# The lo parts of tiles 4 to 7 of the second norm made by GpSimd, with a search of 63 rounds for the order

## The chip, the cores and the metric

The kernel runs on one core of a Trainium2 chip. The metric is the device time of one execution in microseconds (us). The kernel before takes 686.99 us, the median of three runs (686.92 to 687.37). One execution was recorded by the hardware profiler; it took 687.41 us, of which the recorded span is 685.7.

## The reference

One transformer layer on 2048 tokens of width 448: attention over a sliding window of 256 tokens with 16 heads of 28, behind a layer norm, and a gated feed-forward part of inner width 1792, behind a second layer norm. Both are added to what came in.

```
q, k, v = split(layernorm(x) @ wqkv)            # 16 heads of 28
s = q @ k.T * 28**-0.5                          # kept where 0 <= i - j < 256
h = x + concat(softmax(s) @ v) @ wo             # first residual
n = layernorm(h)                                # the second norm
out = h + (gelu(n @ w_gate) * (n @ w_up)) @ w_down
```

All of it is float32.

## The kernel before

**Products.** TensorE multiplies numbers in a rounded float32 form. Each operand is therefore split into a hi part, the value rounded to that form, and a lo part, the rest; a product is the sum of hi by hi, hi by lo and lo by hi. ScalarE makes a hi part by a copy (`to_hi`, L498). VectorE or GpSimd makes the lo part by a subtraction (`to_lo`, L501). All split products are recorded at one line, L495.

**Stages.** The tokens lie in 16 tiles of 128, and `hres` holds the residual stream, which becomes h and then the output. After the first norm and the projections comes attention, in two passes over the heads and 16 blocks of 128 tokens in each: products of scores (L495), maxima on VectorE (`scores`, L924), exponentials on ScalarE (`probs`, L996), the mask on GpSimd (`select`, L1007), products with the values (`attend`, L1026), the division by the sums (`drain`, L1049, on GpSimd in some blocks), the split of a block's output into hi and lo (into `ohl`), its product with `wo`, and the residual add into `hres` (L1073). Blocks end one after the other, and while the later ones are still at work, the second norm of the earlier tiles and the first products of the feed-forward part begin.

**The second norm** (`layer_norms` L515, `normalise` L542, `turn` L583). For each tile VectorE takes the statistics (L530, L532), ScalarE normalises (L548), VectorE transposes in 32 by 32 blocks (L587), and four DMAs on SyncE's queue write the tile to DRAM so that it comes out transposed (L591; the buffers are called xn_122 for tile 0, xn_123 for tile 1, and so on, xn_126 for tile 4 and xn_127 for tile 5). For tiles 0 to 7 two more DMAs bring it back into `xT` (L595, L597), ScalarE makes its hi part (L601 to L603) and an engine its lo part, in two subtractions: 128 by 3 by 128, and 64 by 128 for the last 64 rows of the width, whose hi part is kept in a piece of `ring`. That engine is GpSimd for the tiles listed in `TURNED`, VectorE otherwise (L599). Tiles 8 to 15 are not split there.

**The first products.** `conv` (L1305) makes one inner tile of 128 features for 512 tokens: products of `xT` with weights in `proj`, a gelu (L1339) on ScalarE and a product with the up part (L1341) on VectorE, which goes into `v` and `mt` and is split in turn. `FIRST` lists the eight of these that come first. The pairs in it are (c, k), c the group of 512 tokens: c = 0 needs tiles 0 to 3, c = 1 needs tiles 4 to 7. `down` (L1278) multiplies the results with the down weights and adds them to `hres` (L1296), four tiles a step.

**The units.** The other products go by a scheme with fewer multiplications: `unit` (L1222) uses sums and differences of tiles and of weights. `combine` (L648) makes the combined inputs: it loads transposed tiles from DRAM into `v` (L674), adds or subtracts two of them (L693), and splits the result into hi (ScalarE) and lo (VectorE, X at L501). Its weights come from DRAM, already or not yet combined, and `record` (L1147) handles them, with DMAs at L1157 and L1158 and sums on GpSimd (L1164).

**What sets the order.** No engine's row is written by hand. Each operation is given to a planner (class `Lists`) with its engine, an estimated cost, what it reads and writes, and a key. `run` simulates six queues (TensorE, VectorE, ScalarE, GpSimd, SyncE and a bookkeeping one) and picks on each the operation that can go next by its key. `refine` (L337) repeats this `ROUNDS` times from a fixed random seed: it changes the keys at random, or by how late each operation may start, plans again, and keeps the best by its own estimate. The order kept is then issued. The cost of a lo part in that estimate depends on its engine (L611): 1.6 on GpSimd, 0.75 on VectorE. Another cost or engine for one operation, or another number of rounds, gives another order nearly everywhere. PSUM has eight banks, which the planner hands out as well; in the rows below they are bank_138 to bank_145.

Of the kernel before, what the change touches and what calls it, by code (L numbers as in the profile page):

```python
# [51 lines left out]
POOLED = (3,)  # L52
PKX = (2, 3)
MOVED = 0
TURNED = (0, 1, 2, 3)
LN2 = (120, 10)
XK = ((0, 10), (240, 10))
ADDS = ("dve", "dve")
# [14 lines left out]
    return max(n / 2400 + 0.004, 0.112)  # L73


ROUNDS = 110
SEED = 3
HEAT = 0.3
MIX = 0.8
# [17 lines left out]
class Lists:  # L97
# [6 lines left out]
    def op(self, eng, cost, lat, key, fn, r=(), w=(), bank=None, port=False, size=0, tag=None, after=()):  # L104
        o = Op()
        o.eng, o.cost, o.lat, o.key, o.fn, o.port, o.size, o.tag = eng, cost, lat, key, fn, port, size, tag
        o.deps, o.users, o.ready, o.start = set(after), [], 0.0, None
        o.banks = () if bank is None else tuple(bank) if type(bank) is list else (bank,)
        for b in o.banks:
            b.left += 1  # L110
        if eng == "pe":
            w = (*w, *o.banks)
        else:
            r = (*r, *o.banks)
        for toks, wr in ((r, False), (w, True)):
            for tok in toks:
                name, lo, hi = tok if type(tok) is tuple and tok[0] in SPANS else (tok, 0, 1)
                old = self.seen.setdefault(name, [])
                keep = []
                for a in old:  # L120
                    if a[0] < hi and lo < a[1] and a[2] is not o:
                        if wr or a[3]:
                            o.deps.add(a[2])
                        if wr and lo <= a[0] and a[1] <= hi:
                            continue
                    keep.append(a)
                keep.append((lo, hi, o, wr))
                self.seen[name] = keep
        for d in o.deps:
            d.users.append(o)  # L130
        self.ops.append(o)
        if tag is not None:
            self.open[tag] = self.open.get(tag, 0) + 1
            self.all.setdefault(tag, []).append(o)
        return o
# [201 lines left out]
    def refine(self, allowed, idle):  # L337
# [8 lines left out]
        kept = keys = [o.key for o in self.ops]  # L346
        for r in range(ROUNDS):
            kind = rnd.random()
# [28 lines left out]
def block_kernel(ctx: ExitStack, tc, x, wqk_in, wv_in, wo_in, ffn_in, halves_in, out):  # L377
# [77 lines left out]
    def span(name, lo, n):  # L455
        return (name, lo, lo + n)
# [18 lines left out]
    def XT(t):  # L475
        return span("xT", t, 1)
# [106 lines left out]
    def turn(t, key):  # L583
# [14 lines left out]

        eng = nc.gpsimd if t in TURNED else nc.vector  # L599

# [5 lines left out]
        def lo():  # L606
# [3 lines left out]
        op("act", 0.7, 0.82, key + 0.2, hi, [("xt3", t)], [XT(t), span("ring", 10240, 128)])  # L610
        op("pool" if t in TURNED else "dve", 1.6 if t in TURNED else 0.75, 1.7 if t in TURNED else 0.82, key + 0.2, lo,  # L611
           [XT(t), span("ring", 10240, 128)], [XT(t)], port=True)
# [1021 lines left out]
```

## Time and profile before

| what | us |
|---|---|
| median of three runs | 686.99 (686.92 to 687.37) |
| the profiled execution | 687.41 |
| its span | 685.7 |
| TensorE busy | 673.9 (98%), 4079 products |
| VectorE busy | 502.4 (73%) |
| ScalarE busy | 419.6 (61%) |
| GpSimd busy | 296.8 (43%) |

Attention ends some 280 us into the span; the first early product of the feed-forward part starts shortly before, the units run from about 400 us to the end. In the rows, L and a number is a line of the kernel, x and a number a count of instructions, PE is TensorE, DVE is VectorE, ACT is ScalarE, POOL is GpSimd, and SPq is the time in which SyncE's queue held a transfer back. In a row of a timeline the first number is the start in us and the second the busy time of the whole row; what stands in brackets is a wait ahead of it and what ended it. In a row of groups of instructions the three numbers after the count are the shortest, middle and longest in ns, and then the time from the first to the last in us. A list of waits gives the total in us, the count and the longest.

### The profile page before, as it was taken

Reading aid. Unit: us, or ns where it says so; the run is one execution under the profiler, and the core shown is the slowest. Engines: PE = TensorE matmul, PEld = TensorE weight load, DVE = VectorE, ACT = ScalarE, POOL = GpSimd, SP = SyncE. Lnnn points to the kernel's source line nnn. Section 1 sums busy time; section 2 is a strip of 40 time slices with the busy share of each in tenths; the row PEclk is TensorE's granted clock in tenths of the full one; section 3 lists DMA queues with packets and bytes.
Section 4 is the critical chain, followed back from the end, with each engine's and each line's share of the span. In section 5 each row is a group of like instructions: output and inputs, shape, how many; then the busy total and the mean of one; then the engine's idle time right before and its main releaser. Section 6 shows DMA issues by size and latency. Waiting matters only on the chain.

```text
span 685.7 us, 12258 instructions
## 1 busy us (share of the span) xinstructions
PE 673.9 (98%) x4079; PEld 593.4 (87%) x4079; DVE 502.4 (73%) x1274; ACT 419.6 (61%) x908; POOL 296.8 (43%) x462
## 2 busy tenths in 40 slices
PE   8999999999999999999999999999999999999997
PEld 8898888888888877677898899899999999999997
DVE  7968978866587867784899998877667745645544
ACT  7758767777766789696655665644554543533331
POOL 5702544344445668546524465254664631501100
PEclk9999999999999999999999999999999999999999
DMA  8798765566547687633533432212212210111102
GB/s 290 229 307 264 225 186 177 165 191 197 174 149 221 171 245 195 168 74 85 148 91 101 116 110 75 86 53 76 66 53 90 67 53 14 39 53 67 54 1 107
DMA packets 92951, 89.67 MB, mean 131 GB/s; under 512 B 35224, under 2 KB 82008, under 8 KB 92888
## 3 DMA queue, kind: packets, MB, share of 16 engines
q1 hardware_dynamic: 92888, 88.89, 43.4%
q8 instruction: 32, 0.52, 0.3%
q14 instruction: 31, 0.25, 0.1%
HBM read 59.51 MB, written 29.36 MB: 130 GB/s over the span
## 4 chain that ended last, share of the span: by engine, by line
PE 86%; DVE 7%; ACT 3%; DMA 3%; issue 1%; POOL 0%; SPq 0%; DVEq 0%; ACTq 0%
PE bank L495 79%; PE bank L1026 6%; DMA v<-xn 1%; ACT ring L498 1%; PE bank L553 1%; DVE proj L501 1%; DVE v L693 1%; DVE X L501 1%; DVE mt L924 1%; DVE hres L1296 1%; DMA q<-proj 1%; ACT proj L498 1%; ACT xT L498 1%; ACT pp L996 1%; DVE bnst L530 0%
## 5 line engine op out<-in xcount | busy, mean ns | idle before, releaser
L495 PE MATMUL bank<-xT,proj 128*128 128x512 f32 x620 | 178.9, 387 | 0.0
L495 PE MATMUL bank<-ring 84*128 84x384 f32 (+5 forms) x618 | 155.4, 314 | 2.6 <-ACT pp L996 1.5
L924 DVE CUSTOM_DVE_ANT_0 mt<-bank,mt 128x384 bf16<-128x384 f32 (+2 forms) x256 | 129.0, 526 | 36.9 <-PE bank L495 31.9
L996 ACT ACTIVATE pp<-bank 128x384 f32<-128x384 f32 (+2 forms) x352 | 123.6, 390 | 45.1 <-PE bank L495 41.7
L495 PE MATMUL bank<-xT,ring 128*128 128x512 f32 x536 | 134.9, 380 | 0.1
L495 PEld LDWEIGHTS bank<-ring 104*128 104x128 f32 (+2 forms) x618 | 109.8, 191 | 25.6 <-issue 5.6
L495 PE MATMUL bank<-ring,proj 128*128 128x448 f32 x628 | 127.5, 353 | 1.6 <-DVE hres L1296 1.6
L1007 POOL TENSOR_SCALAR_AFFINE_SELECT pp<-pp 128x512 f32<-128x512 f32 x120 | 74.9, 638 | 117.2 <-ACT pp L996 106.1
L495 PEld LDWEIGHTS bank<-xT,proj 128*128 128x128 f32 x620 | 114.4, 191 | 10.8 <-issue 0.6
L495 PEld LDWEIGHTS bank<-ring,proj 128*128 128x128 f32 x628 | 118.6, 189 | 4.6 <-ACT xT L498 1.9
L495 PEld LDWEIGHTS bank<-xT,ring 128*128 128x128 f32 x536 | 100.9, 189 | 13.5 <-DVE v L1240 0.5
L1296 DVE TENSOR_TENSOR hres<-bank,hres 128x448 f32<-128x448 f32 x72 | 41.3, 622 | 26.8 <-PE bank L495 26.7
L495 PE MATMUL bank<-proj,xT 128*128 128x224 f32 x352 | 59.9, 275 | 0.2 <-ACT proj L498 0.2
L1258 ACT ACTIVATE v<-v 128x512 f32<-128x512 f32 x24 | 15.2, 632 | 69.5 <-DVE v L1240 69.5
L501 POOL TENSOR_TENSOR ring<-raw,ring 128x256 fp32r<-128x256 f32 (+2 forms) x42 | 38.3, 921 | 42.1 <-ACT ring L498 34.3
L495 PEld LDWEIGHTS bank<-proj,xT 128*128 128x128 f32 x352 | 53.2, 191 | 1.5 <-ACT proj L498 0.4
L1164 POOL TENSOR_TENSOR v<-raw 128x256 f32<-128x256 f32 x18 | 15.4, 856 | 89.8 <-DMA raw<-in_halves_dram 54.9
L495 PE MATMUL bank<-wos,ohl 128*128 128x448 f32 x192 | 50.2, 363 | 0.0
L501 DVE TENSOR_TENSOR proj<-v,proj 128x512 fp32r<-128x512 f32 (+1 forms) x56 | 43.0, 773 | 8.6 <-ACT proj L498 7.4
L498 ACT ACTIVATE proj<-v 128x512 fp32r<-128x512 f32 (+1 forms) x56 | 33.6, 603 | 24.3 <-DVE v L1266 13.4
L495 PE MATMUL bank<-X,ring 128*128 128x512 f32 x146 | 48.2, 379 | 0.0
L1164 POOL TENSOR_TENSOR raw<-raw 64x128 f32<-64x128 f32 (+1 forms) x90 | 46.1, 525 | 2.2
(116 smaller groups left out, 987.5 us busy)
## 6 DMA issues: line engine op xcount, KB each, us to landing
ring<-k SPq DMA_DIRECT2D x44, 336.0 KB
raw<-in_halves_dram SPq DMA_DIRECT2D x18, 640.0 KB
ring<-q SPq DMA_DIRECT2D x32, 336.0 KB
q<-proj SPq DMA_DIRECT2D x15, 448.0 KB
k<-proj SPq DMA_DIRECT2D x11, 448.0 KB
hres<-in_x_dram SPq DMA_DIRECT2D x16, 224.0 KB
xn<-xn SPq DMA_DIRECT2D x64, 56.0 KB
mt<-in_halves_dram SPq DMA_DIRECT2D x16, 224.0 KB
```

The source lines that it names most:

```text
L495: nc.tensor.matmul(o.rearrange("p (t h) -> p t h", h=2), w, mixed(m), **how)
L498: nc.scalar.activation(dst, src, AF.Copy)
L501: (eng or nc.vector).tensor_sub(dst, src, f(hi))
L553: nc.tensor.transpose(bank[b.k][:, n * 128:(n + 1) * 128], xn[i2][:, o:o + 128], ident)
L693: op("dve", 0.07 + n * 0.00104, 0.17 + n * 0.00104, key, lambda: nc.vector.tensor_tensor(out, a, b, op=op_), [*ar, *br, "mtfree"], w, port ...
L924: nc.vector.tensor_tensor_reduce(plain(junk[s % 2][:, o:384]), unmixed(bank[b.k][:, o:384]), plain(mask[:, o:384]), 1.0, -BIG, OP.add, OP. ...
L996: nc.scalar.activation(plain(pp[:, j, o * 128:o * 128 + n]), unmixed(bank[b.k][:, 0:n]), AF.Exp, scale=SCALE)
L1007: nc.gpsimd.affine_select(a, a, pattern=[[0, 4], [-cm, 128]], compare_op=op_, fill=0.0, base=0, channel_multiplier=cm)
L1026: nc.tensor.matmul(bank[b.k][32 * j:32 * j + DH + 1, lo * 128:(hi + 1) * 128], v[:, 4 * c - 2 + m, g % 2, j, :], pp[:, j, at[m] * 128:(at[ ...
L1164: op("pool", 0.14 + n * 0.00215, 0.18 + n * 0.00215, key, lambda: nc.gpsimd.tensor_tensor(out, a, b, op=OP.subtract), [*ar, *br], w, port= ...
L1258: op("act", 0.485, 0.608, key + 11, lambda: nc.scalar.activation(A, A, AF.Gelu_apprx_tanh), ta, ta)
L1296: op("dve", 0.533, 0.626, key + 3 * q + 3, lambda t=t, b=banks[q]: nc.vector.tensor_tensor(plain(hres[:, t, :]), unmixed(bank[b.k][:, 0:D] ...
```

## The change

The list of tiles whose lo part GpSimd makes grows from tiles 0 to 3 to tiles 0 to 7, and the search for the order has 63 rounds and not 110.

```diff
@@ -52,7 +52,7 @@
 POOLED = (3,)
 PKX = (2, 3)
 MOVED = 0
-TURNED = (0, 1, 2, 3)
+TURNED = (0, 1, 2, 3, 4, 5, 6, 7)
 LN2 = (120, 10)
@@ -73,7 +73,7 @@
-ROUNDS = 110
+ROUNDS = 63
 SEED = 3
```

Eight instructions change their engine: the two subtractions of tiles 4, 5, 6 and 7. None is added or taken away. The order changes on every engine; the three places on which the prediction rests follow.

GpSimd at the end of attention, before. `pp` are the exponentials, `oblk` a block's output, `ohl` its split:

```order
L1007 AFFINE_SELECT pp<-pp 128x4x128 x3
L1049 TENSOR_TENSOR oblk<-oblk,rcp_87 128x512
L1007 AFFINE_SELECT pp<-pp 128x4x128 x2
L501 TENSOR_TENSOR ohl<-oT,ohl 128x512
L1007 AFFINE_SELECT pp<-pp 128x4x128 x5
```

And the same place of the changed kernel:

```order
L1007 AFFINE_SELECT pp<-pp 128x4x128 x4
L1049 TENSOR_TENSOR oblk<-oblk,rcp_87 128x512
L1007 AFFINE_SELECT pp<-pp 128x4x128 x2
L501 TENSOR_TENSOR xT<-xT 128x3x128
L501 TENSOR_TENSOR xT<-xT,ring 64x128
L501 TENSOR_TENSOR ohl<-oT,ohl 128x512
L1007 AFFINE_SELECT pp<-pp 128x4x128 x2
L501 TENSOR_TENSOR xT<-xT 128x3x128
L501 TENSOR_TENSOR xT<-xT,ring 64x128
```

The lo parts of tiles 4 and 5 now stand between the selections. Those of tiles 6 and 7 follow further down in the same manner, tile 7's between two selections of the last block; VectorE's row has none of the four pairs left.

VectorE at the first step of `down`, before. The adds at L1073 are the last residual adds of attention, `v` and `mt` at L1341 the products with the up part, and `proj<-v,proj` the lo part of the first such product:

```order
L1073 TENSOR_TENSOR hres<-bank_144,hres 128x448
L1341 TENSOR_TENSOR v<-v 128x512 x2
L1073 TENSOR_TENSOR hres<-bank_142,hres 128x448
L1073 TENSOR_TENSOR hres<-bank_145,hres 128x448
L1341 TENSOR_TENSOR mt<-bank_139,mt 128x512
L1073 TENSOR_TENSOR hres<-bank_144,hres 128x448
L530 BN_STATS bnst_80<-hres 128x6
L501 TENSOR_TENSOR proj<-v,proj 128x512
```

And in the changed kernel:

```order
L1073 TENSOR_TENSOR hres<-bank_144,hres 128x448
L1341 TENSOR_TENSOR v<-v 128x512 x2
L1073 TENSOR_TENSOR hres<-bank_145,hres 128x448
L501 TENSOR_TENSOR proj<-v,proj 128x512
L1073 TENSOR_TENSOR hres<-bank_142,hres 128x448
L1073 TENSOR_TENSOR hres<-bank_144,hres 128x448
L1341 TENSOR_TENSOR mt<-bank_139,mt 128x512
L530 BN_STATS bnst_80<-hres 128x6
L532 BN_AGGR bnmv<-bnst_80 128x2
L501 TENSOR_TENSOR proj<-v,proj 128x512
```

The first lo split stands behind one residual add there and not behind three adds, a product and a statistics step; the second split stands where the first one stood.

SyncE, on which all DMAs are issued, at the loads for the first combined inputs, before:

```order
L674 DMA v<-xn_126 64x128
L674 DMA v<-xn_126 128x2x128
L1158 DMA v<-in_halves_dram 128x448
L674 DMA v<-xn_126 64x2x128
L674 DMA v<-xn_127 64x128
L674 DMA v<-xn_122 64x2x128
L674 DMA v<-xn_122 128x2x128
L674 DMA v<-xn_127 128x2x128
L1157 DMA raw<-in_halves_dram 128x1280
L674 DMA v<-xn_126 64x2x128
L674 DMA v<-xn_127 64x2x128
L674 DMA v<-xn_122 64x2x128
```

And in the changed kernel:

```order
L674 DMA v<-xn_126 64x128
L674 DMA v<-xn_126 128x2x128
L1158 DMA v<-in_halves_dram 128x448
L674 DMA v<-xn_122 64x2x128
L674 DMA v<-xn_122 128x2x128
L674 DMA v<-xn_126 64x2x128
L674 DMA v<-xn_127 64x128
L674 DMA v<-xn_127 128x2x128
L674 DMA v<-xn_122 64x2x128
```

The third load of tile 0 (the last row of both) stands ahead of the weight record (L1157), which comes five rows further down in the changed kernel.

## The prediction

> **What bounds the kernel now.** I read the page first: the engines' totals, and the chain that ended last.
>
> ```profile
> span 685.7 us, 12258 instructions
> PE 673.9 (98%) x4079; PEld 593.4 (87%) x4079; DVE 502.4 (73%) x1274; ACT 419.6 (61%) x908; POOL 296.8 (43%) x462
> PE 86%; DVE 7%; ACT 3%; DMA 3%; issue 1%; POOL 0%; SPq 0%; DVEq 0%; ACTq 0%
> ```
>
> TensorE is the bound: 98% busy and 86% of the chain. The change takes no product away, so it can gain only where TensorE stands still or runs slowly. Where that is, TensorE's own waits and a table by stage tell.
>
> ```profile
> PE bank L495 <- DVE proj L501: 1.7, 1, 1.7
> PE bank L495 <- DVE hres L1296: 1.6, 1, 1.6
> PE bank L495 <- ACT pp L996: 1.5, 4, 0.8
> 275.00:280.00 5.00, 3.95 (x21) 2.65 (x18) 4.86 (x20) 3.37 (x11) 4.32 (x7) 1.00 0.98 285
> 280.00:284.00 4.00, 4.00 (x15) 3.29 (x14) 1.76 (x9) 1.38 (x4) 1.84 (x5) 0.57 1.00 234
> 284.00:300.00 16.00, 16.00 (x118) 12.29 (x118) 13.52 (x46) 14.13 (x38) 6.62 (x9) 1.00 0.34 74
> 300.00:320.00 20.00, 19.71 (x140) 15.48 (x143) 11.26 (x26) 17.18 (x44) 13.20 (x21) 1.00 0.33 63
> 320.00:340.00 20.00, 18.34 (x106) 16.59 (x99) 15.87 (x31) 10.30 (x17) 7.91 (x11) 1.00 0.56 158
> 340.00:360.00 20.00, 20.00 (x99) 18.36 (x98) 18.75 (x52) 12.24 (x24) 7.64 (x14) 1.00 0.32 85
> 360.00:380.00 20.00, 18.42 (x91) 16.68 (x90) 18.91 (x43) 10.43 (x18) 7.71 (x11) 1.00 0.40 107
> 400.00:560.00 160.00, 160.00 (x780) 146.79 (x778) 121.00 (x209) 85.50 (x156) 82.26 (x128) 1.00 0.23 72
> ```
>
> After each stage and its length stand the busy times of TensorE, its weight loads, VectorE, ScalarE and GpSimd, and then the granted clock. Four things are to be seen. The second half runs without a gap (160.00 of 160). Two single waits of 1.7 and 1.6, both for VectorE, lie in 320 to 340 and 360 to 380. At the end of attention TensorE misses 1.05 in 275 to 280, with VectorE busy 4.86 of 5 and GpSimd 4.32, and right behind it the clock is 0.57 over 4 us: (1 - 0.57) x 4 = 1.7 us lost. And in 284 to 320, where VectorE still makes the lo parts of tiles 4 to 7, TensorE misses 0.29.
>
> **The change part by part.** *The moved lo parts.* Each is two subtractions; their prices on both engines:
>
> ```profile
> L501 POOL TENSOR_TENSOR xT<-xT x4: 1002/1004/1009, 241.4 to 277.1; 128x384 fp32r<-128x384 f32 x4
> L501 POOL TENSOR_TENSOR xT<-xT,ring x4: 454/456/462, 242.5 to 278.2; 64x128 fp32r<-64x128 f32 x4
> L501 DVE TENSOR_TENSOR xT<-xT x4: 547/552/559, 294.7 to 310.9; 128x384 fp32r<-128x384 f32 x4
> L501 DVE TENSOR_TENSOR xT<-xT,ring x4: 290/290/318, 295.3 to 311.5; 64x128 fp32r<-64x128 f32 x4
> ```
>
> VectorE loses 4 x (0.55 + 0.29) = 3.4 us and GpSimd gains 4 x (1.00 + 0.46) = 5.8. Both fall in 290 to 312. VectorE is busy there 13.52 of 16 and 11.26 of 20, so its release is worth at most the 0.29 that TensorE misses. GpSimd goes from 6.62 + 13.20 = 19.8 busy of 36 to 25.6: room on the average. In the new order ScalarE's hi part of tile 4 comes ahead of the last hi split of block 13's output, and the lo part stands behind two selections, so GpSimd need not idle for it. Only at the end is it tight, with tile 7:
>
> ```profile
> 311.51 0.29 DVE L501 TENSOR_TENSOR xT<-xT,ring 64x128 fp32r<-64x128 f32 x1
> ...
> 312.76 1.56 PE L495 MATMUL bank<-xT,proj 128*128 128x512 f32 x6
> ```
>
> The lo part ends at 311.80 and its first product starts at 312.76: 0.96 of cover, of which the slower engine takes (1.00 + 0.46) - (0.55 + 0.29) = 0.6. I cost this at nothing; if GpSimd's queue is late by more than 0.36, the products of tiles 4 to 7 are the next thing late. Ends: -0.3 (VectorE's release counts) and +5.8 (all four lo parts on the path).
>
> *The stretch before the first early product.* The new search moves nearly every row. Ahead of the lo part of tile 3, which that product waits for, stand the same GpSimd instructions in both orders, only in another sequence; TensorE has two score products more ahead of the early product. So I take 0. Its ends: -1.05 - 1.7 = -2.7, if wait and slow clock both go, and as much to the other side.
>
> *The start.* There the trace shows VectorE's steps up to the lo part of tile 3:
>
> ```profile
> 9.12 0.69 DVE L501 TENSOR_TENSOR proj<-raw,proj 128x512 fp32r<-128x512 f32 x1
> ...
> 10.74 0.63 DVE L530 BATCH_NORM_STATS2 bnst<-hres 128x6 f32<-128x448 f32 x1
> ```
>
> The new order has a second such weight split ahead of it and not this statistics step: +0.06, taken as 0. Ends: one such step either way, 0.7.
>
> *The first wait of the feed-forward part.* Here the order bears more than the moved work does.
>
> ```profile
> 329.10 0.35 PE L495 MATMUL bank<-proj 128*128 128x448 f32 x1
> 331.11 2.73 PE L495 MATMUL bank<-proj 128*128 128x448 f32 x13 [1.66 <-DVE proj L501]
> 326.44 1.28 DVE L1341 TENSOR_TENSOR v<-v 128x512 f32<-128x512 f32 x2
> 327.64 1.15 DVE L1073 TENSOR_TENSOR hres<-bank,hres 128x448 f32<-128x448 f32 x2
> ...
> 329.30 0.62 DVE L1073 TENSOR_TENSOR hres<-bank,hres 128x448 f32<-128x448 f32 x1
> ...
> 330.37 0.68 DVE L501 TENSOR_TENSOR proj<-v,proj 128x512 fp32r<-128x512 f32 x1
> 327.50 1.14 ACT L498 ACTIVATE proj<-v 128x512 fp32r<-128x512 f32 x2
> ```
>
> The second product of the first down step waits for a lo split that VectorE starts at 330.37, behind three residual adds, a product and a statistics step. Its hi part on ScalarE is done about 328.1. In the new order the split stands right behind the first add: that add ends near 328.2, the split takes 0.68 and is done at 328.9, ahead of the product at 329.1. What is late next is that step's first bank: it now belongs to the add behind the split, which ends at 328.9 + 0.6 = 329.5. So 0.4 of the wait stays, and 0.1 comes at the second step, whose split now has a product and a statistics step less of a head start: -1.66 + 0.5 = -1.2. Ends: -1.66, and -0.6 if ScalarE's part is late by one of its steps of 0.6.
>
> *The second wait.* VectorE is behind here (18.75 and 18.91 of 20):
>
> ```profile
> 361.37 2.43 PE L495 MATMUL bank<-ring,proj 128*128 128x448 f32 x12
> 365.38 2.51 PE L495 MATMUL bank<-ring,proj 128*128 128x448 f32 x12 [1.58 <-DVE hres L1296]
> 363.29 0.42 DVE L501 TENSOR_TENSOR X<-v,xT 128x256 fp32r<-128x256 f32 x1
> 363.62 0.48 DVE L693 TENSOR_TENSOR v<-v 64x128 f32<-64x128 f32 x2
> ...
> 364.63 2.20 DVE L1296 TENSOR_TENSOR hres<-bank,hres 128x448 f32<-128x448 f32 x4
> 334.14 0.60 SPq L674
> ...
> 334.80 4.82 DMA v<-xn
> ...
> 339.63 0.64 ACT xT L498
> 340.36 0.63 DVE L501 TENSOR_TENSOR X<-v,xT 128x128 fp32r<-128x128 f32 x2 [2.11 <-ACT xT L498]
> ```
>
> The four residual adds of a down step start at 364.63, some 2.4 after the first three of the twelve products (361.37 + 0.6 + drain). Three changes meet. Five VectorE steps stand behind these adds now and not ahead (the three shown, 0.9 together, and two more of that size: 1.5). The wait of 2.11 at 340.36 is for the combined input of tile 0, whose last transfer SyncE issued at 334.14. Its buffer is free when the lo split above is done, now 328.9 and not 331.05; and the new order issues this transfer ahead of the 640 KB weight record, not behind it. I take 1.7 of the 2.11 as saved (ends 0 and 2.11). Against these, TensorE comes 1.2 earlier. VectorE is then 2.4 - 1.5 - 1.7 + 1.2 = 0.4 late, which the other nine products cover. But the five steps are still owed before the first unit's products, and VectorE has no other slack: together the two waits can give little more than the 1.7 it saves and 0.2 of play. So the second gives 1.9 - 1.2 = 0.7 of its 1.58. Ends: 0, -1.58.
>
> *Behind.* 0: the next 160 us hide everything.
>
> **Sum**: 0 + 0 + 0 - 1.2 - 0.7 = -1.9. The profiled execution took 687.41 (685.7 and 1.7 around it): 685.5. It lies 0.4 above the median of the runs, 686.99, which gives **685.1**.
>
> **The rivals.** *Slower: GpSimd's queue.* The lo parts stand ahead of selections, and every attend product waits for selections. For it: GpSimd takes 1.46 for each, in order. Against it: GpSimd now mostly waits for the exponentials. If two of the four come onto the path, 2 x 1.46 = 2.9; TensorE then waits longer than the 1.05 after which the clock fell, and I add another 1.7 for that: 687.0 - 1.9 + 2.9 + 1.7 = 689.7. It decides from 1.9 us of added wait.
>
> *No change.* The transfer of 4.82 takes as long in its new place, and VectorE's wait stays. What is gained at 329 is then waited for at 365: 687.0.
>
> *More gain: the clock.* TensorE fell to 0.57 after missing 1.05 of 5 us in several pieces, and did not after the single waits of 1.66 and 1.58. If the new order fills 275 to 280 better, 1.7 goes too: 687.0 - 1.9 - 1.7 = 683.4. [...]
>
> **How the numbers follow.** Forecast 0.45 (with its ends 683.6 to 686.6), slower 0.23, no change 0.17, clock 0.15. The range 682.6 to 689.4 takes in the clock case and most of the slow one, and leaves out the sums of all ends. A change below 0.2% (1.4 us) is about what a measurement of this kernel cannot tell. Faster by more: three quarters of the forecast and the clock case, 0.34 + 0.15 = 0.49. Within: 0.11 of the forecast and 0.15 of no change, 0.26. Slower: the rest, 0.25.
>
> **What would show it.** In the changed profile: TensorE's wait for the split of the first down step at most 0.5; VectorE's wait before the first combined input below 1; no wait of more than 0.9 for the residual adds; TensorE's miss in the 36 us of tiles 4 to 7 still below 0.5; one slow stretch of the clock. I am wrong if attend products wait for GpSimd, if the products of tiles 4 to 7 start late, or if the slow stretch comes twice or not at all.

## The result: slower, by the order and not by the engine

The changed kernel takes 690.19 us (689.82 to 691.26), the kernel before 686.99 (686.02 to 687.37) beside it: 3.2 us more by the medians. The ratio is 1.0055, with a 95% interval of 1.0040 to 1.0071, or 3.8 us (2.7 to 4.9). The forecast was 685.1, the range 682.6 to 689.4.

The head of the page of the changed kernel's profiled execution (690.96 us, span 689.2):

```profile
span 689.2 us, 12270 instructions
PE 677.1 (98%) x4077; PEld 592.6 (86%) x4077; DVE 497.9 (72%) x1266; ACT 420.5 (61%) x908; POOL 307.0 (45%) x470
PE 84%; DVE 7%; ACT 3%; DMA 2%; issue 2%; SPq 1%; DVEq 0%; ACTq 0%
```

VectorE lost 4.5 us of work and GpSimd gained 10.2 (its count grew by 8), where 3.4 and 5.8 were forecast. In the two experiments below that take the change apart, the moved work alone gives GpSimd 5.4 more (302.2 us), and the new order alone 5.0 more with the same instructions (301.8 us). TensorE is the bound as before. Its waits, as total, count and longest:

```profile
PE bank L495 <- DVE mx L924: 1.6, 6, 0.4
PE bank L951 <- DVE mhl L944: 1.3, 2, 0.7
PE bank L495 <- DVE xT L501: 0.9, 1, 0.9
PE bank L495 <- DVE hres L1296: 0.8, 1, 0.8
PE bank L495 <- DVE hres L1073: 0.3, 1, 0.3
```

The wait of 1.7 for the split of the first down step is gone and the one of 1.6 for the residual adds is halved, as forecast. The waits for maxima (mx) grew from 0.6 in two pieces to 1.6 in six. New are those for VectorE's small step behind the maxima (mhl) and one for a lo part of the first norm (xT at the top of the kernel). The table by stage, with the columns of the prediction (length; busy time of TensorE, weight loads, VectorE, ScalarE, GpSimd; granted clock; DMA share and rate):

```profile
275.00:280.00 5.00, 4.72 (x42) 3.39 (x41) 4.83 (x17) 3.67 (x9) 4.84 (x8) 1.00 0.46 142
280.00:284.00 4.00, 2.85 (x12) 1.86 (x11) 3.71 (x13) 2.97 (x11) 3.46 (x4) 0.88 0.73 152
284.00:300.00 16.00, 15.40 (x102) 11.58 (x101) 9.79 (x36) 11.87 (x28) 8.89 (x15) 0.82 0.47 120
300.00:320.00 20.00, 18.69 (x132) 14.59 (x132) 12.25 (x33) 17.22 (x45) 14.49 (x27) 1.00 0.35 71
320.00:340.00 20.00, 19.73 (x117) 17.28 (x117) 12.12 (x23) 11.95 (x25) 11.04 (x11) 1.00 0.39 104
360.00:380.00 20.00, 19.25 (x96) 17.58 (x95) 19.29 (x47) 11.15 (x20) 9.41 (x14) 1.00 0.32 97
```

From 320 on TensorE misses 0.27 + 0.75 where it missed 1.66 + 1.58: the two gains are there. But at the end of attention it misses 1.15 of 4 and then runs at 0.82 over 16 us: 0.12 x 4 + 0.18 x 16 = 3.4 us lost to the clock, twice the 1.7 of before. And in 284 to 320 it misses 0.60 + 1.31 = 1.91, before 0.29.

**The end of attention, row by row.** What TensorE could have done in its gaps are the first early products. In the kernel before they started at 279.91:

```profile
279.91 1.44 PE L495 MATMUL bank<-xT,proj 128*128 128x512 f32 x4
```

In the changed kernel the lo part of tile 3 starts on GpSimd at 282.62 and the first early product at 283.89, while TensorE, by an estimate from the starts of its products up to 260 us, was only some 3 us behind the kernel before:

```profile
281.52 0.52 ACT L498 ACTIVATE xT<-xT 128x384 fp32r<-128x384 f32 x1
...
281.39 1.27 POOL L501 TENSOR_TENSOR ohl<-oT,ohl 128x512 fp32r<-128x512 f32 x1 [0.46 <-ACT ohl L498]
282.62 0.99 POOL L501 TENSOR_TENSOR xT<-xT 128x384 fp32r<-128x384 f32 x1
...
283.89 0.63 PE L495 MATMUL bank<-xT,proj 128*128 128x512 f32 x1
285.12 0.35 PE L951 MATMUL bank<-one,mhl 128*72 128x128 f32 x1 [0.60 <-DVE mhl L944]
```

So TensorE had only score products there, and four of them waited for VectorE's maxima to free a bank. The lo part stood behind the split of a block's output on GpSimd, but its own hi part was done on ScalarE only at 282.04 (281.52 + 0.52). Its place on GpSimd therefore explains at most 0.6 of the 5.5 us by which it started later than before (277.12).

**One place where the moved work stands in the way** in this execution is at 302.6:

```profile
302.58 1.00 POOL L501 TENSOR_TENSOR xT<-xT 128x384 fp32r<-128x384 f32 x1 [0.92 <-ACT xT L498]
302.61 0.98 DVE L944 SCALAR_TENSOR_TENSOR mhl<-mx,mhl 128x8 fp32r<-128x8 f32 x1
303.75 0.25 PE L951 MATMUL bank<-one,mhl 128*72 128x128 f32 x1 [0.69 <-DVE mhl L944]
```

VectorE's small step, 0.17 us in the median of its 32, starts 0.03 behind GpSimd's subtraction for tile 5 and ends with it (303.59 and 303.58); TensorE waits 0.69 for it. The moved work is not needed for such a meeting. In the kernel before, the same step takes as long (1.03) beside another of GpSimd's subtractions and ends with that one (81.18 and 81.15), and TensorE does not wait for it there:

```profile
80.15 1.03 DVE L944 SCALAR_TENSOR_TENSOR mhl<-mx,mhl 128x8 fp32r<-128x8 f32 x1
...
80.02 1.13 POOL L501 TENSOR_TENSOR wos<-raw,wos 128x448 fp32r<-128x448 f32 x1
```

### The profile page after: what moved, and what is told of

It is laid out like the page before. It is cut to its first block, busy times and chain, and to the rows that moved or that the text cites. A ratio compares the mean times of both kernels' runs of the same rounds, so it can differ in the third digit from the quotient of the medians.

```text
span 689.2 us, 12270 instructions
## 1 busy us (share of the span) xinstructions
PE 677.1 (98%) x4077; PEld 592.6 (86%) x4077; DVE 497.9 (72%) x1266; ACT 420.5 (61%) x908; POOL 307.0 (45%) x470
## 4 chain that ended last, share of the span: by engine, by line
PE 84%; DVE 7%; ACT 3%; DMA 2%; issue 2%; SPq 1%; DVEq 0%; ACTq 0%
PE bank L495 78%; PE bank L1026 5%; ACT pp L996 1%; DVE mt L924 1%; DVE proj L501 1%; DMA pp<-in_wv_dram 1%; DVE xT L501 1%; DVE bnst L530 1%; DVE X L501 1%; DMA hres<-in_x_dram 1%; ACT ring L498 1%; ACT proj L498 0%; SPq L674 0%; ACT xT L498 0%; PE bank L951 0%
## 5 line engine op out<-in xcount | busy, mean ns | idle before, releaser
L495 PE MATMUL bank<-xT,proj 128*128 128x512 f32 x620 | 176.4, 389 | 1.0 <-DVE xT L501 0.9
L495 PE MATMUL bank<-ring 84*128 84x384 f32 (+6 forms) x618 | 153.3, 316 | 2.8 <-DVE mx L924 1.6
L495 PEld LDWEIGHTS bank<-ring 104*128 104x128 f32 (+2 forms) x618 | 108.2, 191 | 24.7 <-ACT pp L996 5.7
L1007 POOL TENSOR_SCALAR_AFFINE_SELECT pp<-pp 128x512 f32<-128x512 f32 x120 | 76.4, 650 | 114.1 <-ACT pp L996 112.6
L501 DVE TENSOR_TENSOR proj<-v,proj 128x512 fp32r<-128x512 f32 (+1 forms) x56 | 42.6, 765 | 10.2 <-ACT proj L498 8.8
```

The source lines that it names most:

```text
L495: nc.tensor.matmul(o.rearrange("p (t h) -> p t h", h=2), w, mixed(m), **how)
L501: (eng or nc.vector).tensor_sub(dst, src, f(hi))
L1007: nc.gpsimd.affine_select(a, a, pattern=[[0, 4], [-cm, 128]], compare_op=op_, fill=0.0, base=0, channel_multiplier=cm)
```

## The experiments

Two theories: O, the order that the search found is worse; G, the work on GpSimd itself costs. A table by kernel stands at the end of this section. "Lost to the clock" there is (1 - mean granted clock) x time, averaged over a kernel's executions.

**The two parts apart.** The first kernel keeps the order of before and changes the engine alone:

```diff
-        eng = nc.gpsimd if t in TURNED else nc.vector
+        eng = nc.gpsimd
```

> The order of the kernel before, row for row, and GpSimd in place of VectorE for the lo parts of tiles 4 to 7, at the same places. Theory O (the other order made it slower, not the engine): 686.8 to 687.8, since GpSimd's lo parts can at most hold VectorE up in a few places. Rival G (the work on GpSimd itself made it slower): 689 to 690.5, close to the changed kernel.

Measured: 686.83, ratio 1.0003 (0.9991 to 1.0016). The second keeps the order of the changed kernel and puts the four lo parts back:

```diff
-        eng = nc.gpsimd if t in TURNED else nc.vector
+        eng = nc.gpsimd if t < 4 else nc.vector
```

> The order of the changed kernel, row for row, with the lo parts of tiles 4 to 7 on VectorE again. Theory O: 689.2 to 690.2; only the wait of 0.7 at 303 us, where VectorE's step was held up while GpSimd made a lo part, goes. Rival G: 686 to 687.5.

Measured: 689.90, ratio 1.0041 (1.0027 to 1.0054). G falls in both directions: the order costs 2.8 us (1.9 to 3.7), and what the engine costs lies within about 1 us of nothing, too little for these runs to tell. The third draws another order without moving work:

```diff
-ROUNDS = 110
+ROUNDS = 63
```

> The kernel before with a search of 63 rounds: no work changes its engine, the order is another one. Theory O: such a draw moves the time by 1 to 3 us either way, so more than 0.7 from 687.0. Rival G: without the moved work the time stays within 0.7 of 687.0.

Measured: 687.48, ratio 1.0004 (0.9993 to 1.0015). The total did not move by more than 0.7, so what O expected of it failed; but its parts moved: 0.2 lost to the clock in place of 1.7, and 1.6 more in the rest. (For eight tiles, 63 and 110 rounds give the same order, row for row; the number of rounds by itself does nothing to the changed kernel.)

**Where the order costs, by splices.** Each engine's row is made of the rows of one kernel up to a time and of the other's behind it (the time is the planner's estimate of the start, which lies within a few us of the profile). In the cut, `b` is the order of before and `a` that of the changed kernel; the dots stand for the lines that plan both:

```diff
-    L.refine(allowed, idle)
-    L.run(allowed, idle, True)
...
+    first, last = plans["b"][2], plans["a"][2]
+    early = {o for o, s in zip(L.ops, plans["b"][1]) if s < 322.5}
+    seq = [o for o in first if o in early] + [o for o in last if o not in early]
+    L.force = {e: [o for o in seq if o.eng == e] for e in ("py", "pe", "dve", "act", "pool", "sp")}
+    assert L.run(allowed, idle, True)
```

Before up to 322 us, the changed kernel behind it, all lo parts on the engines of before:

> The order of the kernel before up to the last residual adds of attention (some 322 us), lo parts of tiles 4 to 7 on VectorE; from there the order of the changed kernel. If the two gains forecast behind 322 us belong to that order: 687.0 - 2.1 = 684.9 (684.3 to 685.6). Rival: the stretch behind 322 us looked better only because TensorE came to it late and VectorE had caught up: 686.6 to 687.4.

Measured: 684.95, ratio 0.9965 (0.9951 to 0.9980), faster than both kernels. The gains behind 322 us belong to that order; they are not owed to TensorE being late. The same splice with the four lo parts on GpSimd:

> The spliced order (684.95) with the lo parts of tiles 4 to 7 on GpSimd. Theory O: the engine is worth nothing either way: 684.9 (684.4 to 685.5). Rival G: GpSimd in the way costs 1 or more: 686 and above.

Measured: 685.31, ratio 0.9964 (0.9949 to 0.9979): again no cost of the engine. With the seam at 248 us, so that the end of attention comes from the changed kernel too:

> The order of the kernel before for the first 248 us, from there that of the changed kernel, with GpSimd. Against the splice at 322 us (684.95) it takes over the end of attention of the changed kernel as well. Theory: that stretch costs 0.8 of waits at 280 us, 0.9 at tiles 4 to 7 and 1.5 of slow clock: 688.2 (687.4 to 689.0). Rival: the loss at the end of attention is only owed to what TensorE, VectorE and GpSimd bring along from before 248 us: 685 to 686.

Measured: 687.43, ratio 0.9997 (0.9984 to 1.0010). The time is at the lower edge of what the theory expected; the ratio, 686.8 us, lies between theory and rival. That stretch costs some 2.3 us (0.9997 against 0.9964), and its table shows gaps at the same place as in the changed kernel (1.20 of 5 missing; there 1.62), with the slow clock in them:

```profile
280.00:285.00 5.00, 3.80 (x13) 2.94 (x13) 3.15 (x14) 1.66 (x4) 3.34 (x8) 0.71 0.93 276
```

By the ratios the rest of the loss lies ahead of 248. The other way round, the changed kernel's first 45 us ahead of the order of before:

> The order of the changed kernel for the first 45 us, from there that of the kernel before; lo parts of tiles 4 to 7 on VectorE. Theory: the start costs the 1.2 that TensorE lost up to 30 us: 687.0 + 1.2 = 688.2 (687.8 to 688.7). Rival: it is caught up in attention: 686.9 to 687.4.

Measured: 687.80, ratio 1.0006 (0.9989 to 1.0023). The time is at the theory's lower edge, the ratio (687.4) at the rival's upper one, so the run does not decide. In its profiled execution the start is not caught up in attention: the first early product starts 1.66 later than before (279.91).

```profile
281.57 1.03 PE L495 MATMUL bank<-xT,proj 128*128 128x512 f32 x4
```

That execution ended near the time of the kernel before all the same: it kept full clock at 280 to 284 (0.999 in the mean of the execution), where the other lost 1.7. With the changed kernel's first 250 us ahead of the order of before:

> The order of the changed kernel for the first 250 us, from there that of the kernel before, with the end of attention of the kernel before. Theory: the start (1.2) and the many small losses of the first 240 us (1.2 by the two profiled executions) add up: 689.4 (688.6 to 690.2). Rival: the small losses are chance between two executions: 688.2, as with the start alone.

Measured: 691.35, ratio 1.0082 (1.0057 to 1.0107). More than either expected. In its profile TensorE misses 1.01 of 4 at 250 to 254 and runs at a slow clock from 254 to 260, right behind the seam (mean clock of that execution 0.993). Neither kernel has that, so the seam itself costs something and this run settles nothing. Three more seams with the order of before ahead:

> The order of the kernel before for the first 58 us, from there that of the changed kernel, with GpSimd. Theory (spread): the small waits of the weight loads in attention (8.9 in all between 35 and 250 us, before 5.0) are spread evenly; only the start and a fifth of the rest go: 689.9 (689.3 to 690.5). Rival (start): most of the 3 us arises ahead of 58 us: 687.4 to 688.4.

> The same with the seam at 100 us. Theory (spread): a further 0.8 goes against the seam at 58: 689.1 (688.5 to 689.7). Rival (one place, 100 to 248 us): as with the seam at 58.

> The same with the seam at 180 us. Theory (spread): a further 0.8 to 1 goes: 688.2 (687.6 to 688.8). Rival (one place, 180 to 248 us): 689 and above, as with the seam at 100.

Measured: 694.32 at 58 us (ratio 1.0108, 1.0090 to 1.0125), 690.21 at 100 (1.0060, 1.0037 to 1.0083) and 687.55 at 180 (1.0007, 0.9994 to 1.0020). The first is spoiled by its seam too: TensorE waits 2.4 us in one piece for a maximum at 60 us. The seam at 100 gave neither expected number. The seam at 180 came out at the theory's lower edge, against its rival, and gives within 0.7 us the time of the seam at 248. So some 3 us of the loss lie ahead of 180 us (1.0051 and 1.0055 against 1.0007), the start included. How they divide is not settled, since a seam can cost something of its own. By the ratios all of it lies behind 100 us. By an estimate from the starts of TensorE's products in the profiled execution, TensorE falls behind by some 1.1 us up to 35, by 1.2 more up to 100 and by 1.1 more up to 180.

**What it is made of there.** TensorE's own row shows next to nothing between 35 and 100 us, for before and after alike:

```profile
35.00:100.00 65.00, 64.94 (x480) 56.03 (x479) 51.34 (x183) 46.49 (x114) 20.93 (x30) 1.00 0.78 250
```

```profile
35.00:100.00 65.00, 64.92 (x457) 55.13 (x460) 51.42 (x187) 45.91 (x111) 21.00 (x31) 1.00 0.76 235
```

It got through 480 products in the one and 457 in the other, of another mixture, with 0.06 and 0.08 us missing. The row hides short waits, because a product's busy time reaches over the next one's. Here twelve products of the changed kernel at 369 us, with a mean of 359 ns each, are busy for 2.5 us together and not for 4.3:

```profile
L495 PE MATMUL bank<-ring,proj 128*128 128x448 f32 x12 | 2.5, 359 | 0.8 <-DVE hres L1296 0.8
```

The waits of its weight loads (PEld) between 35 and 250 us differ; of before:

```profile
PEld bank L495 <- ACT ring L498: 1.0, 2, 0.6
PEld bank L495 <- ACT pp L996: 0.6, 3, 0.3
...
PEld bank L495 <- DVE proj L501: 0.6, 1, 0.6
...
PEld bank L495 <- DVE mx L924: 0.2, 1, 0.2
```

Of the changed kernel:

```profile
PEld bank L495 <- ACT pp L996: 2.9, 13, 0.4
...
PEld bank L495 <- DVE proj L501: 2.3, 4, 0.6
...
PEld bank L495 <- DVE mx L924: 0.9, 5, 0.2
```

Thirteen short waits for banks from which ScalarE still takes exponentials, four for lo splits, five for maxima: 9.3 us of waits for engines in all against 5.0. A second profiled execution of the changed kernel has the same counts. That these waits are the loss is not shown. No run took them away one by one, and they do not divide as the loss does: of the some 4 us more, 2.2 lie ahead of 100 us, 0.6 between 100 and 180 and 1.4 behind 180. The run with the seam at 180 has 4.2 us of them behind 180, more than the changed kernel (3.6), and still takes within 0.7 us the time of the run with the seam at 248. What makes the loss ahead of 180 us stays open. In the two rows above the busy time of the products is equal (64.94 and 64.92 of 65); the difference stands in the waits of the weight loads.

**Single places of the changed kernel.** At the start TensorE waited 0.88 for a lo part behind a copy on VectorE that took 1.79 us in place of 0.56; GpSimd cleared memory meanwhile:

```profile
27.15 1.79 DVE L800 CAST ring<-e 8x768 fp32r<-8x768 f32 x1
28.95 0.87 DVE L501 TENSOR_TENSOR xT<-bank,xT 128x384 fp32r<-128x384 f32 x2
...
27.58 0.94 POOL L794 MEMSET ring<- 32x1024 f32 x1
...
29.87 4.46 PE L495 MATMUL bank<-xT,proj 128*128 128x512 f32 x19 [0.88 <-DVE xT L501]
```

The copy (operation 230 of the order) was put behind that lo part (operation 240):

```diff
...
+    for a, b in ((230, 240),):
+        r = lanes[seq[a].eng]
+        r.remove(seq[a])
+        r.insert(r.index(seq[b]) + 1, seq[a])
...
```

> The changed kernel with one instruction of VectorE's row moved: the copy of 1.79 us at 27.15 us (which ends only after GpSimd's last clearing) goes behind the lo part of tile 7 that TensorE waited for. Theory: the 0.9 that TensorE waited there comes off, and nothing behind takes it back: 689.2 (688.8 to 689.6). Rival: attention behind it is held by other engines and gives it back: 690.0 to 690.4.

Measured: 690.18, ratio 1.0044 (1.0026 to 1.0062). The wait is gone from the profile. The time is the rival's, the ratio 0.5 to 0.8 us below the changed kernel's, and the intervals of both are too wide to tell the theory's 1.0 from nothing. Besides, the profiled execution of the order alone, which has the same rows there, has the same copy at 0.91 and no such wait. There the copy ends 0.42 behind the first of two clearings (28.31 and 27.89), in the changed kernel 0.42 behind the second (28.94 and 28.52): this differed between executions of the same rows. Then the end of attention, with the hi and lo part of tile 3 earlier and five early products between the score products (the lines below this one are those of the cut above):

```diff
+    for a, b in ((2797, 2750), (2808, 2777), (2817, 2792), (2819, 2798), (2822, 2801), (2824, 2806), (2825, 2810)):
...
```

> The changed kernel with seven operations moved at 277 to 287 us: the hi part of tile 3 on ScalarE and its lo part on GpSimd some 4 us earlier, and the first five early products on TensorE put between the last score products of block 14, where it waited. Theory: the 1.1 of TensorE's waits at 280 to 284 is filled, and with fewer gaps the slow clock (two stretches, 3.4 lost) comes once or not at all: 690.2 - 1.1 - 1.7 = 687.4 (686.0 to 688.2). Rival: the slow clock has nothing to do with the gaps: 689.1 (688.7 to 689.6).

Measured: 689.18, ratio 1.0025 (1.0012 to 1.0039), near the number of the rival, but not for its reason. TensorE's gaps were not filled:

```profile
280.00:285.00 5.00, 3.38 (x16) 2.52 (x16) 4.71 (x18) 1.93 (x8) 3.98 (x6) 1.00 0.67 150
```

It misses 1.6 of 5 as before the edit. The early products did run from 281.50 on, but VectorE was busy 4.71 of 5 as it was without the edit, and TensorE then waited 0.99 for its small step behind the maxima (0.60 without the edit). What fell is the loss to the clock, from 3.2 to 1.2. So my reading, fill the gap and win twice, failed in its first half.

**The clock.** The changed kernel once more, for its clock:

> The changed kernel once more, beside the others, for its mean granted clock. Theory: two slow stretches at the end of attention belong to its order: clock 0.9955 in the mean (3.1 lost) against 0.9976 of the kernel before (1.6 lost), 690.2 (689.6 to 690.8). Rival: its five runs were chance: clock as before, 688.7.

Measured: 691.19, ratio 1.0051 (1.0036 to 1.0067), mean clock 0.9953: the loss to the clock belongs to its order. In this execution the two slow stretches stand apart, each behind a stretch with gaps: TensorE misses 1.71 of 5 in 270 to 275 and 1.35 of 5 in 285 to 290. Then a gap made on purpose, in the order that had nearly no loss to the clock:

```diff
-... lambda t=t: nc.vector.bn_stats(bnst[t % 2], hres[:, t, :]), ...
+... lambda t=t: [nc.vector.bn_stats(bnst[t % 2], hres[:, t, :]) for _ in range(4 if (kind, t) == ("ln2", 6) else 1)], ...
```

> The order of the kernel before found with 63 rounds (687.5; granted clock 0.9997 in the mean of its runs, so 0.2 lost to the slow clock), and VectorE takes the statistics of tile 6 four times in place of once, at 275 us, between the maxima of block 14: 1.6 of work more, for which TensorE then waits. Theory: the gaps bring the slow clock; lost to it 1.2 to 2 in place of 0.2, and 1.0 to 1.6 of waits: 690.0 (689.4 to 691). Rival: the slow clock has nothing to do with gaps there: lost 0.2 as without them, 688.8 (688.3 to 689.1).

Measured: 689.87, ratio 1.0034 (1.0023 to 1.0046). The order without the added work, and below it with the work (the same stage):

```profile
275.00:280.00 5.00, 4.70 (x29) 3.92 (x30) 4.74 (x17) 4.92 (x14) 4.38 (x10) 1.00 0.49 139
```

```profile
275.00:280.00 5.00, 3.60 (x25) 2.88 (x21) 4.90 (x16) 3.22 (x9) 4.09 (x8) 1.00 0.49 139
```

TensorE misses 1.40 in place of 0.30. Lost to the clock are 1.0 in the mean in place of 0.2, less than the 1.2 to 2 expected, and the other 1.6 are lost to the waits. The gap brings the slow clock, though not in every execution: the one shown kept full clock, five of the twelve did not (0.998 or less), and without the gap none of twelve fell below 0.999. The two kernels ran on two different chips, between which the mean clock of the kernel before differed by 0.0005.

| kernel | ratio to before (95%) | mean clock | lost to the clock, us |
|---|---|---|---|
| before (100 executions beside the others) | 1 | 0.9976 | 1.7 |
| changed, two sets | 1.0055 and 1.0051 | 0.9953 | 3.2 |
| engine alone | 1.0003 (0.9991, 1.0016) | 0.9976 | 1.6 |
| order alone | 1.0041 (1.0027, 1.0054) | 0.9958 | 2.9 |
| 63 rounds, engines of before | 1.0004 (0.9993, 1.0015) | 0.9997 | 0.2 |
| the same with the gap | 1.0034 (1.0023, 1.0046) | 0.9986 | 1.0 |
| changed from 322 us on | 0.9965 (0.9951, 0.9980) | 0.9975 | 1.7 |
| changed from 322 us on, GpSimd | 0.9964 (0.9949, 0.9979) | 0.9970 | 2.1 |
| changed from 248 us on | 0.9997 (0.9984, 1.0010) | 0.9961 | 2.7 |
| changed from 180 us on | 1.0007 (0.9994, 1.0020) | 0.9955 | 3.1 |
| changed from 100 us on | 1.0060 (1.0037, 1.0083) | 0.9950 | 3.5 |
| changed from 58 us on | 1.0108 (1.0090, 1.0125) | 0.9927 | 5.1 |
| changed up to 45 us | 1.0006 (0.9989, 1.0023) | 0.9971 | 2.0 |
| changed up to 250 us | 1.0082 (1.0057, 1.0107) | 0.9966 | 2.3 |
| changed, copy moved | 1.0044 (1.0026, 1.0062) | 0.9960 | 2.8 |
| changed, early products moved | 1.0025 (1.0012, 1.0039) | 0.9982 | 1.2 |

By the rows of the seams at 180 and 322 us, the changed kernel's loss is put together of some 3 us ahead of 180 us, some 3 between 180 and 322 us (1.0007 against 0.9964, about a third of it clock), and a gain of 2.5 behind. That the three can be added up is assumed; each has an interval of about 1 us to either side.

## Why the prediction was wrong, point by point

**The moved lo parts: right.** Cost at nothing; engine alone 1.0003, and 0.9964 against 0.9965 in the splice. The far end of +5.8 was never near. TensorE's miss in the 36 us of tiles 4 to 7 was to stay below 0.5 and came to 1.91; with the order alone it is 0.42 + 0.95 = 1.37, so most of that is the order. No product of tiles 4 to 7 waits for GpSimd in the changed profile. The rival "GpSimd's queue" gave 689.7, close to the measured 690.2, but by a mechanism that these runs rule out. That it came so near was luck. GpSimd's queue did come late in one place: VectorE waits 2.96 for the division of a block's output, which stands on GpSimd behind the lo part of tile 6, where it waits 1.17 with the order alone. No wait of TensorE follows from it.

```profile
314.95 0.71 DVE L1054 STREAM_TRANSPOSE oT<-oblk 128x512 f32<-128x512 f32 x1 [2.96 <-POOL oblk L1049]
```

What I had not named is that the moved work can also hurt by VectorE's step beside it (0.98 in place of 0.17). In the rows at 302.6 the step ends with GpSimd's subtraction, and so it does in those of the kernel before at 80 (1.03); it happened once on TensorE's path, and no run shows it in the total.

**The first wait of the feed-forward part: right.** I left 0.4 of it, for an add behind the split, and 0.1 at the second step. Measured: 0.27, for just that add, in the changed kernel and in the splice:

```profile
335.70 4.78 PE L495 MATMUL bank<-proj 128*128 128x448 f32 x24 [0.27 <-DVE hres L1073]
```

**The second wait: right in kind.** VectorE's wait of 2.11 before the first combined input is gone (0.3 is left ahead of the step before it), as forecast. Of TensorE's wait 0.9 was to be left; it is 0.75 in the changed kernel, where TensorE comes late, and 1.40 and 0.98 in the two splices, where it does not:

```profile
362.11 2.51 PE L495 MATMUL bank<-ring,proj 128*128 128x448 f32 x12 [1.40 <-DVE hres L1296]
...
362.18 2.51 PE L495 MATMUL bank<-ring,proj 128*128 128x448 f32 x12 [0.98 <-DVE hres L1296]
```

The sum of both terms, -1.9, stands against -2.4 measured for the order behind 322 us (0.35% of 687), whose interval is -3.4 to -1.4. By the rows the two waits give 1.6 and 2.0 of it; the rest is not traced.

**The stretch before the first early product: wrong.** It was taken as 0 with ends of 2.7 either way, because the same GpSimd instructions stand ahead of tile 3's lo part in both orders. They do, but what counts is when they can run: the hi part that this lo part needs came late from ScalarE, and the split of a block's output ahead of it on GpSimd waited for ScalarE too. The lo part started 5.5 us later than before, while TensorE was some 3 later. What in the order made ScalarE late is not shown. The stretch from 248 to 322 us, of which this is the first part, costs 2.3 us by the splices, of which 0.6 to 1.0 is clock; that is nearly the far end of the term's bounds.

**The step that failed most is one that the sum did not have.** "The new search moves nearly every row" stood in the text, and then only the places were priced at which TensorE's row showed a gap or an edit. The prediction held that the change can gain only where TensorE stands still or runs slowly, and read from TensorE's own waits where that is. Attention between 30 and 260 us got no term, neither a gain nor a loss: TensorE is busy there in 19.95 to 20.00 of each 20 us up to 240. Ahead of 180 us the new order cost some 3 us by the splices, long before the first moved lo part (297 us). What holds TensorE up there is not shown. The start belongs to that stretch; whether its term, 0 with ends of 0.7, was in order stays open: the total of its run is 1.0006 (0.9989 to 1.0023), while TensorE was 1.66 late at the first early product.

**The clock.** The rival had it that filling the gaps would spare 1.7; the mechanism went the other way, with more gaps and 1.5 more lost. The slow stretch came twice, one of the signs of being wrong that the prediction had named. With the sum's own gains alone the kernel would have been at 685, as the splice at 322 us was (684.95).

## What to carry to other kernels

Where a change makes a planner or a search draw a new order, the change's own work may be the smallest term: price the order too, and allow a range for it in every stage, also in those where the bounding engine shows no gap. To tell the two apart, run the old order with the new engine and the new order with the old one, and splice the orders by time; the pieces can then be kept one by one, which here gave a kernel faster than both (0.9965). On TensorE read the waits of the weight loads beside those of the products: here, between 35 and 250 us, the first show 5.0 us of waits for engines before and 9.3 in the changed kernel, and the second none in either. They are a hint and not a price: here they did not divide over the kernel as the lost time did.

## What the runs showed of the hardware

The same program differs from execution to execution by its slow clock. Over 100 executions of the kernel before, on four chips, the mean granted clock went from 1.000 (21 executions, 685.7 us in the mean) over 0.998 (26, 687.3) to 0.992 (5, 690.4). The one slow stretch in the profile of the kernel before has a clock of 0.70, 0.50, 0.50 and 0.60 in the four us from 280 to 284, which is 3.4 us at 0.50 and costs 1.7; by an estimate from the mean clocks, executions have none to about three of them. The splice at 322 us has the gaps of the kernel before at 275 to 280, to the hundredth, and no slow clock behind them in its profiled execution:

```profile
275.00:280.00 5.00, 3.95 (x21) 2.65 (x18) 4.86 (x20) 3.35 (x11) 4.31 (x7) 1.00 0.98 281
280.00:284.00 4.00, 4.00 (x25) 3.43 (x24) 3.05 (x15) 2.69 (x8) 1.83 (x5) 1.00 0.95 229
```

So the same gaps came with a slow clock in one execution and without it in another. The longest wait of TensorE behind its first products is 2.4 us, in the run with the seam at 58 us; there the clock is 0.85 in 60 to 62, 0.50 in 62 to 64 and 0.79 in 64 to 66. How large or how dense gaps must be is not settled: 1.40 missing of 5 cost 1.0 in the mean, 1.05 cost 1.7, and the edit at the end of attention left the gaps as they were and the loss fell from 3.2 to 1.2.

A copy on VectorE beside a clearing on GpSimd took 1.79 us in three profiled executions and 0.85 to 0.91 in others, 0.56 where none ran.
